# Sigmoid attention and a gated feed-forward on one core: the last gate on VectorE, sums issued earlier, the last copy in two halves

## The chip, the cores and the metric

The kernel runs on one core of one Trainium2 chip. The metric is the device time of one execution in microseconds (us). The core has five engines, each with an instruction queue of its own that is worked off in order: PE (TensorE, matmuls; its weight loads are the row PEld), DVE (VectorE), ACT (ScalarE), POOL (GpSimd) and SP (SyncE, which here only issues DMAs). An engine waits for another by semaphores. PSUM, which matmuls write, has 8 banks of 512 fp32 columns; SBUF holds everything else.

## The reference

With 8 batches, 12 heads, 448 tokens and a head size of 64, and then 3584 tokens of 768 features and 2048 hidden units:

```python
scores = scale * np.matmul(q, k.transpose(0, 1, 3, 2)) - np.log(S)
attn = 1.0 / (1.0 + np.exp(-scores))
x = np.matmul(attn, v)            # (8, 12, 448, 64), to (3584, 768) by token
h = x @ w_in                      # 768 -> 2048
g = h * (1.0 / (1.0 + np.exp(-beta * h)))
out = g @ w_out                   # 2048 -> 768
```

All inputs and the output are float32.

## The kernel before

Matmuls take fp16 operands. The attention is worked off by groups of four heads (24 groups of two score slots each, three groups to a batch). A **visit** (`visit`, L255) computes one key block's scores of a group: 8 or 16 short matmuls (L217) into four PSUM banks, and one sigmoid over all four (L245, on ACT, 1792 columns) that writes the attention weights to `attns`. The next visit's scores go to the same four banks, so they can start only when that sigmoid has read them. `attend` (L293) multiplies a group's weights with v (L304) and DVE copies the result to `xT` (L313). DVE also transposes q and k of the coming groups (L192, L200, L204), and doubles v's short last block (`double_v_last`, L157).

The two dense layers are the other half of PE's work. The first batches run plainly (`dense1`, `dense2`). From batch 2 on, two batches go together: `blocks(b, ...)` (L495), called for b = 2, 4 and 6 and called a **run** here, computes the first layer of batches b and b+1 by a seven-product Strassen scheme with 8 blocks i = 0..7 (`NB1` is 8). Each block leaves four results of 128 hidden units by 448 tokens. They are named A and B (the first batch, lower and upper half of the hidden units), D and E (the same of the second batch). A, B and D stand in PSUM; E is written by DVE to a scratch place in SBUF, inside `attns` (L553). `whole(key, i)` and `gate` (L486) finish a result: ACT computes the sigmoid into `sg` (L488), and one engine multiplies it with the result into the fp16 hidden tensor `gt` (L491). The multiplication of E is on POOL, that of A, B and D on DVE.

The second layer reads `gt` by tiles of 128 tokens. A run gives 7 tiles (`NTILE`), called a window: three pairs of tiles by seven products each (`strassen`, L584) and one tile alone (`single`, L375). Product i of a pair is 8 matmuls (dc = 0..7, `ND` is 8) of 384 columns, L593. Products 0 and 1 read `gt` itself; products 2 to 6 read a sum of two parts of `gt`, which `hidden_sum` makes on DVE (L582, fp16, 128x1024). The sum for product i+2 is issued within product i, at the matmul that the line L587 names. After products 1 to 6 ACT (L614) or DVE (L611, L616) takes the PSUM result into the output tile `osb`, and `store` (L633) issues its DMAs on SP.

The order of all work is written by hand (`tc.manual_schedule()`); each engine's queue holds its instructions in the order in which the Python code emits them. Matmuls of the dense layers lie in a list, `fill`, of which the main loop spends so many after each visit as a planned pace says. At a run, the main loop puts the new window at the end of `fill` but keeps the 8 last matmuls of the window before for use within the run. At its end, `blocks` emits, in this order:

```python
            if i:                                     # i == NB1 here
                whole("D", i - 1)()
            if i == NB1:
                share_psum(scores)
                other(2)                              # new window: product 0, dc 0 and 1
            if i:
                product1(b, i - 1, 4, kept[i - 1, "B"], False)
            if i:
                whole("B", i - 1)()
        other(ND - 2)                                 # product 0, dc 2 to 7; the sum at dc 4
        whole("E", NB1 - 1)()
```

After that come the visits of the main loop and, with them, products 1, 2 and so on. After the third run there are no visits left, and the second layer of the last window runs through to the end. The tile that comes last is tile 27 (`NT - 1`), which is computed alone: its right half is copied and stored first, its left half (`half == 0`) last, by `leave` (L363).

Of the kernel before, what the change touches and what calls it, by code (L numbers as in the profile page):

```python
# [13 lines left out]
def kernel(  # L14
# [10 lines left out]
    nc = tc.nc  # L25
# [17 lines left out]
    NB1 = DFF // P // 2  # L43
    NDC = DFF // P
    HALF = DM // 2
    WIN = 2 * S
    NTILE = WIN // P
# [25 lines left out]
    def share_psum(sc: int):  # L73

        scored[:] = [(2 * i, 2 * i + 1) for i in range(sc)]
        last = max(used.values())
        for i in range(2 * sc):
            used.pop(i, None)
        for i in range(2 * sc, 8):
            used.setdefault(i, last)  # L80

    def touch(i: int):
        used[i] = max(used.values(), default=0) + 1

    def bank(cols: int = S, hold=None, at=None):
        if at is None:
            at = min((i for i in used if i not in held.values()), key=used.get)
        assert at not in held.values()
        touch(at)
        if hold is not None:  # L90
            held[hold] = at
        width[at] = cols
        return ps[:, at, 0:cols]
# [222 lines left out]
    osbs = {}  # L316
# [27 lines left out]
    def release(key):  # L344
        touch(held.pop(key))
        m2s.pop(key)
# [16 lines left out]
    def leave(t: int, half: int, m2):  # L363
        lo, hi = half * HALF, (half + 1) * HALF
        release((t, half))
        if t not in osbs:
            osbs[t] = outp.tile([P, DM], FP32, tag="osb", name="osb")
        nc.vector.tensor_copy(out=osbs[t][:, lo:hi], in_=m2)
        left[t] = left.get(t, 0) + 1
        if t == NT - 1:  # L370
            store(t, lo, hi)
        elif left[t] == 2:
            store(t, 0, DM)
# [21 lines left out]
    NT = NTOK // P  # L395
# [5 lines left out]
    ND = NDC // 2  # L401
# [37 lines left out]
    def scratch(i: int, n: int):  # L439

        return attns[:, i : i + n].rearrange("p n h s -> p (n h s)")
# [21 lines left out]
    def product1(b: int, i: int, n: int, out, start: bool):  # L463

        x, y = xTs[b], xTs[b + 1]
        t1, t2, t3, t4 = xs[b]
        w, m = (
            (A11, x[:, 0:KH]),
            (A12, x[:, KH:]),
            (us["S4"], y[:, KH:]),  # L470
            (A22, t4),
            (us["S1"], t1),
            (us["S2"], t2),
            (us["S3"], t3),
        )[n - 1]
        for c in range(KH):
            nc.tensor.matmul(  # L477
                out,
                w[:, c, i * P : (i + 1) * P],
                m[:, c],  # L480
                start=(start and c == 0),
                stop=(c == KH - 1),
                skip_group_check=not start,
            )

    def gate(h, dc: int, b: int, engine):  # L486
        sg = sigp.tile([P, S], FP32, tag="sg", name="sg")
        nc.scalar.activation(  # L488
            out=sg, in_=h, func=AF.Sigmoid, bias=0.0, scale=beta_sb[:, dc : dc + 1]
        )  # L490
        return lambda: engine.tensor_tensor(  # L491
            out=gt[:, dc, b % 2 * S : b % 2 * S + S], in0=h, in1=sg, op=ALU.mult
        )

    def blocks(b: int, other, scores: int):  # L495

        kept = {}
        rest = sorted(used, key=used.get)
        firsts = [i for i in rest if width[i] == S and i not in held.values()][:2]
        others = sorted((i for i in rest if i not in firsts), key=lambda i: i in held.values())  # L500
        (b0, d0), (b2, d2) = scored
        share_psum(0)

        def take(key, i):
            at = firsts[i % 2] if key == "A" else ((b0, d0), others, (b2, d2))[i % 3][key == "D"]
            assert key != "A" or width[at] == S
            kept[i, key] = bank(S, (i, key), at)
            return kept[i, key]

        def whole(key, i):  # L510
            h = kept.pop((i, key))
            if (i, key) in held:
                touch(held.pop((i, key)))
            half, second = {"A": (0, 0), "D": (0, 1), "B": (1, 0), "E": (1, 1)}[key]
            return gate(h, i + half * NB1, b + second, nc.gpsimd if key == "E" else nc.vector)

        for i in range(NB1 + 1):
            p5 = scratch(6 + i % 2, 1).bitcast(FP32)
            if i < NB1:
                B = take("B", i)  # L520
                product1(b, i, 1, B, True)
                A = take("A", i)
                nc.scalar.copy(out=A, in_=B)
                D = take("D", i)
                product1(b, i, 5, D, True)
                nc.scalar.copy(out=p5, in_=D)
            if i:
                product1(b, i - 1, 3, kept[i - 1, "D"], False)
            if 0 < i < NB1:
                late = whole("E", i - 1)  # L530
            if i == 0:
                other(ND // 2)
            if i < NB1:
                product1(b, i, 6, B, False)
                nc.vector.tensor_tensor(out=D, in0=B, in1=p5, op=ALU.add)  # L535
            if 0 < i < NB1:
                late()
            if i:
                whole("D", i - 1)()
            if i < NB1:  # L540
                product1(b, i, 2, A, False)
                whole("A", i)()
            if i == 0:
                other(ND // 2)
            if i == NB1:
                share_psum(scores)
                other(2)
            if i:
                product1(b, i - 1, 4, kept[i - 1, "B"], False)
            if i < NB1:  # L550
                product1(b, i, 7, B, False)
                E = kept[i, "E"] = scratch(8 + i % 2, 1).bitcast(FP32)
                nc.vector.tensor_tensor(out=E, in0=B, in1=p5, op=ALU.add)  # L553
            if i:
                whole("B", i - 1)()
        other(ND - 2)
        whole("E", NB1 - 1)()
# [17 lines left out]
    NPROD = 7  # L575
# [8 lines left out]
    def strassen(t: int, i: int, dc: int):  # L584

        name, x, _, op, w = product(t, i)
        if dc == (0 if i else ND // 2) and i + 2 < NPROD:  # L587
            hidden_sum(t, i + 2)
        first = (t, name) not in m2s
        if first:  # L590
            m2s[t, name] = bank(HALF, (t, name))
        m2 = m2s[t, name]
        nc.tensor.matmul(  # L593
            m2,
            (x if op is None else sums[t, i])[:, dc],
            w[:, dc],
            start=first,
            stop=(dc == ND - 1),
            skip_group_check=i >= 4,
        )  # L600
        if dc < ND - 1:
            return
        if i == 0:
            for u in (t, t + 1):
                osbs[u] = outp.tile([P, DM], FP32, tag="osb", name="osb")
        L, R = slice(0, HALF), slice(HALF, DM)
        o1, o2 = osbs[t], osbs[t + 1]
        r, a = m2s.get((t, "r")), m2s.get((t, "a"))

        def add(out, in0, in1, op=ALU.add):  # L610
            nc.vector.tensor_tensor(out=out, in0=in0, in1=in1, op=op)  # L611

        if i == 1:
            nc.scalar.copy(out=o2[:, L], in_=a)  # L614
        elif i == 2:
            nc.vector.tensor_copy(out=o1[:, L], in_=m2)  # L616
            add(o1[:, R], r, o1[:, L])
            release((t, "s"))
        elif i == 3:
            add(o2[:, L], m2, o2[:, L])  # L620
            release((t, "b"))
        elif i == 4:
            add(o2[:, R], a, o2[:, L], ALU.subtract)
        elif i == 5:
            add(o2[:, R], r, o2[:, R])
            release((t, "r"))
            store(t + 1, 0, DM)
        elif i == 6:
            add(o1[:, L], a, o1[:, L], ALU.subtract)
            release((t, "a"))  # L630
            store(t, 0, DM)

    def store(t: int, lo: int, hi: int):  # L633
        osb = osbs[t]
        c, end = t * P, (t + 1) * P
        while c < end:
            b, i = divmod(c, S)
            rows = out[b * S : (b + 1) * S, lo:hi]
            if b == B - 1:
                n = min(end - c, S - i)  # L640
                to = rows[i : i + n]
            else:
                n = BLK
                to = rows.rearrange("(p c) m -> c p m", c=NB)[i // BLK]
            nc.sync.dma_start(out=to, in_=osb[c - t * P : c - t * P + n, lo:hi])
            c += n
# [269 lines left out]
```

## Time and profile before

| | |
|---|---|
| median of 3 runs | 381.13 us (381.05 to 381.13) |
| profiled execution, its own time | 381.19 us |
| its span, from the first to the last instruction | 379.4 us |
| granted TensorE clock | 1.000 |
| PE busy | 370.7 us (98% of the span) |
| DVE busy | 256.8 us (68%) |
| ACT busy | 258.4 us (68%) |
| POOL busy | 94.7 us (25%) |
| runs (first layer of two batches) | 133 to 168, 222 to 257, 309 to 345 us from the span's start |
| last window | 345 to 376 us |

The profile is one execution, taken by the hardware profiler. In its views a row of the timeline has a start and a duration in us, the engine, the line, the operation, what it writes and reads, and how many instructions are merged; in brackets stands how long the engine sat idle before and for whom. Matmuls are pipelined: the record of one ends later than the next begins, so what counts is the distance from start to start. In the view of waits a row reads: who waited, for whom, us in total, times, the longest.

### The profile page before, as it was taken

The page shows a single profiled execution, that of the slowest core. Times are in us where ns is not written, and L with a number is a line of the kernel's source. Part 1 is how long each engine was busy: PE and PEld are TensorE (multiplying, and loading weights), DVE is VectorE, ACT ScalarE, POOL GpSimd, SP SyncE. Part 2 cuts the span into 40 slices and gives each one's busy share as a digit, 9 for nine tenths or more (in the row PEclk, how much of TensorE's full clock was granted, in tenths as well). Part 3 has the DMA queues.
Part 4 walks back from the last instruction along what each step waited for, and adds up shares of the span by engine and source line. Part 5 has one row for each costly group of instructions (what it writes and reads, how often), then busy time and mean ns, then how long its engine had stood idle before and what let it go on. Part 6 is the DMA issues. An engine that isn't in the chain of part 4 may idle for free.

```text
span 379.4 us, 7379 instructions
## 1 busy us (share of the span) xinstructions
PE 370.7 (98%) x2927; PEld 186.2 (49%) x2927; DVE 256.8 (68%) x483; ACT 258.4 (68%) x303; POOL 94.7 (25%) x141
## 2 busy tenths in 40 slices
PE   8999999999999999999999999999999999999996
PEld 3467664444444455544444445554444445555663
DVE  3256686776687786787576666778667567678662
ACT  3987776688977758887767658887677737882000
POOL 7833353141141012335114003227100002231000
PEclk9999999999999999999999999999999999999999
DMA  7999999993339030009739311007903031000333
GB/s 113 177 187 203 197 205 198 214 126 56 50 54 185 18 83 1 2 2 167 152 65 198 76 44 30 2 0 112 194 0 85 7 78 42 2 0 3 83 83 126
DMA packets 42403, 34.31 MB, mean 90 GB/s; under 512 B 21873, under 2 KB 38913, under 8 KB 42369
## 3 DMA queue, kind: packets, MB, share of 16 engines
q0 software_dynamic: 36976, 22.81, 44.2%
q1 hardware_dynamic: 5392, 11.02, 10.3%
q8 instruction: 23, 0.38, 0.4%
q14 instruction: 12, 0.09, 0.1%
HBM read 45.62 MB, written 11.01 MB: 149 GB/s over the span
## 4 chain that ended last, share of the span: by engine, by line
PE 91%; DVE 5%; ACT 3%; issue 1%; ACTq 0%
PE ps L477 25%; PE ps L593 25%; PE ps L217 12%; PE ps L304 10%; PE ps L324 9%; PE ps L353 4%; PE ps L391 4%; PE ps L712 3%; DVE sum L582 1%; ACT attns L230 1%; DVE xT L313 1%; ACT sg L488 1%; DVE ps L535 1%; DVE w_S L437 1%; DVE gt L491 1%
## 5 line engine op out<-in xcount | busy, mean ns | idle before, releaser
L245 ACT ACTIVATE attns<-ps,nlogs 128x1792 f16<-128x1792 f32 x73 | 128.0, 1753 | 49.3 <-PE ps L217 49.1
L491 POOL TENSOR_TENSOR gt<-attns,sg 128x448 f16<-128x448 f32 x24 | 27.3, 1137 | 151.3 <-ACT sg L488 151.3
L593 PEld LDWEIGHTS <-sum 128*128 128x128 f16 x440 | 39.9, 98 | 38.0 <-issue 11.6
L217 PE MATMUL ps<-qT,kT 32*128 32x448 f16 (+3 forms) x864 | 51.8, 340 | 1.3 <-ACT attns L230 0.6
L488 ACT ACTIVATE sg<-ps,beta_sb 128x448 f32<-128x448 f32 x72 | 45.4, 631 | 8.0 <-PE ps L477 5.8
L593 PE MATMUL ps<-w_T,sum 128*128 128x384 f16 x264 | 49.1, 327 | 0.0
L477 PE MATMUL ps<-xT,w_S 128*128 128x448 f16 x216 | 48.7, 352 | 0.2
L477 PE MATMUL ps<-xT,w_in 128*128 128x448 f16 x216 | 48.7, 353 | 0.0
L313 DVE CAST xT<-ps 128x448 f16<-128x448 f32 (+1 forms) x54 | 28.7, 567 | 27.3 <-PE ps L304 27.2
L491 DVE TENSOR_TENSOR gt<-ps,sg 128x448 f16<-128x448 f32 x72 | 44.6, 619 | 1.4 <-ACT sg L488 1.0
L324 PE MATMUL ps<-xT,w_in 128*128 128x224 f16 (+1 forms) x288 | 40.5, 291 | 1.2 <-ACT attns L230 0.8
L304 PE MATMUL ps<-attns,v 128*64 128x448 f16 (+3 forms) x432 | 41.3, 340 | 0.0
L477 PEld LDWEIGHTS <-w_in 128*128 128x128 f16 x288 | 28.0, 98 | 26.3 <-issue 0.4
L611 DVE TENSOR_TENSOR osb<-ps,osb 128x384 f32<-128x384 f32 x55 | 30.5, 555 | 13.2 <-PE ps L593 11.2
L582 DVE TENSOR_TENSOR sum<-gt 128x1024 f16<-128x1024 f16 x55 | 38.9, 729 | 0.2
L126 POOL DMA_DIRECT2D raw<-in_q_dram x27 | 15.0, 557 | 76.5 <-DVE kT L204 66.7
L593 PE MATMUL ps<-w_out,sum 128*128 128x384 f16 x176 | 32.4, 327 | 1.5 <-DVE sum L582 1.1
L338 DVE TENSOR_TENSOR gt<-ps,sg 128x224 f16<-128x224 f32 (+1 forms) x48 | 21.1, 465 | 18.2 <-ACT sg L335 18.2
L593 PE MATMUL ps<-w_out,gt 128*128 128x384 f16 x176 | 33.3, 327 | 0.0
L324 PEld LDWEIGHTS <-w_in 128*128 128x128 f16 x288 | 26.4, 98 | 14.0 <-issue 6.6
L535 DVE TENSOR_TENSOR ps<-ps,attns 128x448 f32<-128x448 f32 x24 | 15.2, 632 | 24.4 <-PE ps L477 24.4
L477 PEld LDWEIGHTS <-w_S 128*128 128x128 f16 x216 | 21.1, 98 | 20.1 <-issue 0.9
(49 smaller groups left out, 376.0 us busy)
## 6 DMA issues: line engine op xcount, KB each, us to landing
out_dram<-osb SPq DMA_DIRECT2D x98, 96.0 KB, 1.9
raw<-in_k_dram POOLq DMA_DIRECT2D x24, 224.0 KB, 5.4
raw<-in_q_dram POOLq DMA_DIRECT2D x21, 224.0 KB, 4.3
v<-in_v_dram POOLq DMA_DIRECT2D x32, 144.0 KB, 6.9
w_in<-in_moe_w_in_dram POOLq DMA_DIRECT2D x8, 384.0 KB, 10.8
w_out<-in_moe_w_out_dram POOLq DMA_DIRECT2D x4, 768.0 KB, 13.6
v<-in_v_dram POOLq DMA_DIRECT2D x16, 48.0 KB, 6.5
out_dram<-osb SPq DMA_DIRECT2D x2, 384.0 KB, 2.6
```

Of the source, the lines that this page charges most:

```text
L217: nc.tensor.matmul(sco[base : base + nk, hh, u0 : u0 + n], kT[g][lo : lo + BLK, jt * P : jt * P + nk, e], qT[g][lo : lo + BLK, c0 : c0 + n ...
L245: nc.scalar.activation(out=attns[:, slot : slot + 2].rearrange("p n h s -> p (n h) s"), in_=sco, func=AF.Sigmoid, bias=nlogs[:, 0:1], scal ...
L304: nc.tensor.matmul(av[hh * D : (hh + 1) * D, 0:n], vs[b][base : base + nk, 2 * (s % NPAIR) + hh, jt], at[base : base + nk, hh, 0:n], start ...
L313: nc.vector.tensor_copy(out=xTs[b][:, s % NPAIR, c0 : c0 + n], in_=av[:, 0:n])
L324: nc.tensor.matmul(m1, w_in16[:, hc, dc * P : (dc + 1) * P], xTs[b][:, hc, c0 : c0 + n], start=(hc == 0), stop=(hc == NHC - 1),)
L338: nc.vector.tensor_tensor(out=gt[:, dc, off : off + n], in0=m1, in1=sg[:, 0:n], op=ALU.mult)
L477: nc.tensor.matmul(out, w[:, c, i * P : (i + 1) * P], m[:, c], start=(start and c == 0), stop=(c == KH - 1), skip_group_check=not start,)
L488: nc.scalar.activation(out=sg, in_=h, func=AF.Sigmoid, bias=0.0, scale=beta_sb[:, dc : dc + 1])
L491: return lambda: engine.tensor_tensor(out=gt[:, dc, b % 2 * S : b % 2 * S + S], in0=h, in1=sg, op=ALU.mult)
L582: nc.vector.tensor_tensor(out=sums[t, i], in0=x, in1=y, op=op)
L593: nc.tensor.matmul(m2, (x if op is None else sums[t, i])[:, dc], w[:, dc], start=first, stop=(dc == ND - 1), skip_group_check=i >= 4,)
L611: nc.vector.tensor_tensor(out=out, in0=in0, in1=in1, op=op)
```

## The change

There are three edits. First, in each run, E of the last block (i = 7) is multiplied on DVE; E of blocks 0 to 6 stays on POOL. It is still emitted at the same place, after the six matmuls and the sum among them. Second, in the pairs that do not open a window, the sum for product 2 is issued at the first matmul of product 0 and no more at its fifth, four matmuls earlier; these are eight pairs (tiles 3, 5, 9, 11, 16, 18, 23 and 25). The pairs that open a window (tiles 7, 14 and 21) keep the fifth. Third, the last PSUM copy of the kernel, 384 columns on DVE, becomes one of 192 columns on DVE and one of 192 columns on ACT; both read the same PSUM bank.

```diff
@@ leave
-        nc.vector.tensor_copy(out=osbs[t][:, lo:hi], in_=m2)
+        if t == NT - 1 and half == 0:
+            mid = HALF // 2
+            nc.vector.tensor_copy(out=osbs[t][:, lo : lo + mid], in_=m2[:, 0:mid])
+            nc.scalar.copy(out=osbs[t][:, lo + mid : hi], in_=m2[:, mid:])
+        else:
+            nc.vector.tensor_copy(out=osbs[t][:, lo:hi], in_=m2)
@@ blocks, whole
-            return gate(h, i + half * NB1, b + second, nc.gpsimd if key == "E" else nc.vector)
+            return gate(h, i + half * NB1, b + second, nc.gpsimd if key == "E" and i < NB1 - 1 else nc.vector)
@@ strassen
-        if dc == (0 if i else ND // 2) and i + 2 < NPROD:
+        if dc == (ND // 2 if i == 0 and t % NTILE == 0 else 0) and i + 2 < NPROD:
             hidden_sum(t, i + 2)
```

## The prediction

> **What bounds the kernel now.** I read the page's chain first: it is PE's, with a small share of DVE in a line of sums.
>
> ```profile
> PE 91%; DVE 5%; ACT 3%; issue 1%; ACTq 0%
> ```
>
> So an edit counts only where it makes PE go on earlier, or shortens what follows PE's last matmul. The waits say where PE waits for sums:
>
> ```profile
> PEld L593 <- DVE sum L582: 2.2, 3, 1.1
> ...
> PE ps L593 <- DVE sum L582: 1.1, 3, 0.8
> ```
>
> Three times in all, of 55 sums. The sums' own line gives the shortest, median and longest duration in ns:
>
> ```profile
> L582 DVE TENSOR_TENSOR sum<-gt x55: 641/683/1620, 103.8 to 367.8; 128x1024 f16<-128x1024 f16 x55
> ```
>
> A few sums take 1.62 us for 0.68. The timeline around the end of the third run shows what lies beside one:
>
> ```profile
> 342.76 2.44 PE L593 MATMUL ps<-w_out,gt 128*128 128x384 f16 x14
> ...
> 343.49 0.66 ACT L488 ACTIVATE sg<-attns,beta_sb 128x448 f32<-128x448 f32 x1
> 343.62 0.62 DVE L491 TENSOR_TENSOR gt<-ps,sg 128x448 f16<-128x448 f32 x1 [0.32 <-ACT sg L488]
> 344.23 1.13 POOL L491 TENSOR_TENSOR gt<-attns,sg 128x448 f16<-128x448 f32 x1 [3.30 <-ACT sg L488]
> 344.28 2.82 DVE L582 TENSOR_TENSOR sum<-gt 128x1024 f16<-128x1024 f16 x3
> ...
> 345.95 6.13 PEld L593 LDWEIGHTS <-sum 128*128 128x128 f16 x39 [1.15 <-DVE sum L582]
> 345.96 2.77 PE L593 MATMUL ps<-w_out,sum 128*128 128x384 f16 x16 [0.76 <-DVE sum L582]
> ```
>
> POOL's multiplication of E starts at 344.23, the sum for product 2 at 344.28. The chain in order of time gives this sum 1.63 us, to 345.91: it ends 0.55 after POOL (345.36), about what a sum takes alone. It looks as if DVE stood still until POOL was done. At the end of the first run the same pair lies among visits (the second run, at 256.56, repeats it to 0.01 us):
>
> ```profile
> 168.11 1.13 POOL L491 TENSOR_TENSOR gt<-attns,sg 128x448 f16<-128x448 f32 x1 [3.31 <-ACT sg L488]
> 168.17 1.62 DVE L582 TENSOR_TENSOR sum<-gt 128x1024 f16<-128x1024 f16 x1
> ...
> 168.22 1.47 PE L593 MATMUL ps<-w_out,gt 128*128 128x384 f16 x8
> 168.34 1.75 ACT L245 ACTIVATE attns<-ps,nlogs 128x1792 f16<-128x1792 f32 x1 [0.31 <-PE ps L217]
> ...
> 169.85 0.66 PE L593 MATMUL ps<-w_out,sum 128*128 128x384 f16 x3 [0.15 <-DVE sum L582]
> ...
> 170.44 0.57 PE L217 MATMUL ps<-qT,kT 32*128 32x448 f16 x8
> ```
>
> Last, prices, by shape:
>
> ```profile
> L491 DVE TENSOR_TENSOR gt<-ps,sg 128x448 f16<-128x448 f32 x72 | 44.6, 619 | 1.4 <-ACT sg L488 1.0
> ...
> L368 DVE COPY osb<-ps 128x384 f32<-128x384 f32 x12 | 6.7, 555 | 13.3 <-PE ps L391 7.7 <-PE ps L353 5.5
> ...
> L313 DVE CAST xT<-ps 128x224 f16<-128x224 f32 x12 | 4.4, 387 | 4.5 <-PE ps L304 4.5
> ```
>
> **E of the last block on DVE: third run.** Matmuls of L593 follow each other every 0.164 us (16 from 345.96 to the next product's start at 348.57). The 14 before the stall therefore fill PE from 342.76 to 345.06, and product 2 starts at 345.96: 0.90 lost. With POOL idle the sum runs 344.28 to 344.96; PE took up its work 0.05 after the sum's end (345.91 to 345.96), so it may start at 345.01 and PE's own 345.06 decides. In the unstalled stream weight loads lead their matmul by some 0.19 (342.57 against 342.76), and this one leads by 0.05 only, so I take 0.02 off: gain **0.88**.
>
> What is late next? The multiplication now follows that sum on DVE, ahead of the sum for product 3. The trace has none on DVE from SBUF; the nearest row is the same instruction with one operand in PSUM, 0.62; POOL's own 1.13 is the far end. Its sigmoid ended at 344.15, so it does not wait. At 0.62: multiplication 344.9 to 345.5, next sum to 346.2, wanted by PE at 345.06 + 8 x 0.164 = 346.37. It fits by 0.1 or so. At 1.13 it would be 0.4 late and the gain 0.5. I take 0.62. Below 0.62 nothing more is gained. No reader is near: E belongs to the second batch, which the window's second pair opens, 56 matmuls later.
>
> **First and second run.** The 8 matmuls from 168.22 end their turn at 169.53, the sum would be there at 168.85, PE went on at 169.85: 0.32, and 0.31 in the second run (257.98 against 258.29). Behind it waits the next visit, whose scores need the banks that ACT's sigmoid reads until 168.34 + 1.75 = 170.09. PE would get there at 170.44 - 0.32 = 170.12, just after. From then on ACT and PE turn in step: the second sigmoid, at 171.07, waited for those scores, moves with them, and frees the third visit, so I count the gain as carried on: **0.31 twice**. On DVE the k transposes and the sum for product 3 stand behind the multiplication. Before, they stood behind 1.62 us; now behind 0.68 + 0.62 = 1.30, so they are 0.3 early, as PE is. On POOL the next q and k loads stood behind the multiplication (one begins at 169.19, without a wait) and can go after block 6's E (ends 164.81), some 4 us earlier. The DVE work there multiplies fp32 from PSUM and ran beside POOL's earlier E gates at its usual 0.62, so I price this at nothing; if a DVE row were held for one 0.55 us issue per run, PE still would not wait for it.
>
> **Sums four matmuls earlier.** Outside the three places PE never waits for a sum, so there is nothing to gain. In the trace's order only matmuls lie between the first and fifth matmul in five of the eight pairs, and in tile 3's pair a visit without DVE work: the DVE queue stays as it is. In two (visits at 197.94 and 286.25) the doubling of v's last block (0.35) stands there and now comes one sum, 0.68, later; the products with that v come at 211.66 and 299.22, over 12 us on. Without that cover it would cost up to 2 x 0.68; I take **0**. No DMA moves with it.
>
> **The last copy.** A DVE copy is 0.555 for 384 columns; the casts' 0.619 for 448 and 0.387 for 224 give 1.04 ns a column, so 192 take 0.36. ACT's copies are 0.517 for 448 (L523) and 0.474 for 384 (L614): 0.67 ns a column, 0.35 for 192. Side by side the stage shrinks from 0.56 to 0.36: gain 0.20. One after the other, with 0.03 between as from ACT's sigmoid to DVE's multiplication, it is 0.74: loss 0.18. Nowhere in this trace do both engines read one bank at once: ACT's sigmoid and DVE's multiplication of a block follow each other (342.96 + 0.63, then 343.62). That is by their data, but it is the nearest row, and I take the loss, **-0.18**, with both ends kept. The two DMAs now wait for ACT too; the wait is in the 0.18.
>
> The Trainium skill's page "PSUM — Partial Sum Buffer", section "PSUM bank collisions raise a hardware error", speaks against this edit: two engines on one bank and the same partitions at once, two reads included, collide, the hardware doesn't arbitrate, so they have to be kept apart by semaphores. By that rule the sum would hold -0.18, without it +0.20; no row here shows such an overlap.
>
> **Sum.** 0.88 + 0.62 + 0 - 0.18 = 1.32 us. The profiled execution took 381.19 (379.4 of span and 1.8 around it), 0.06 above the median of the runs: 379.87 for it, **379.8** against the median of 381.13.
>
> **Rivals.**
>
> *The halves run side by side* (0.30): 381.13 - 1.70 = 379.4. For it: they write different columns and neither needs the other. Against: the missing overlap.
>
> *The first two gains are not carried on* (0.08). Visits are close to ACT's limit: scores at 172.87 start 0.05 after the sigmoid's end (171.07 + 1.75). If the turn between them doesn't shift, 0.62 is lost: 380.4 (380.05 with parallel halves). Against it: just there ACT waited for PE.
>
> *The sum stays long* (0.07), because something other than POOL holds it. Then the multiplication only lengthens DVE's queue, the sum for product 3 ends at about 347.2, before PE wants it (347.27): 381.1 to 381.3. Against: the three long sums are the three with POOL beside them, to the same 0.06 us.
>
> *DVE blocked behind ACT: slower* (0.05). A gate on DVE blocks everything behind it if its sigmoid is late. Were that sigmoid queued behind the visit's 1.75 us one, it would end at 170.09 + 0.67 = 170.76; multiplication 0.62, k transposes 0.57 and 0.20, sum 0.68: 172.83, while PE wants that sum at 171.46 (5 matmuls after the visit, which ends at 170.64). PE stalls 1.4 and nets 1.1 lost in each of two runs: 381.13 + 2.2 - 0.88 + 0.18 = 382.6. It decides once the sigmoid ends after about 169.4. Against: it is issued before the visit and starts at 167.38.
>
> **How the numbers follow.** The forecast has 0.50. A measurement of this kernel can tell about 0.2%, 0.76 us. The forecast, the parallel halves and a third of the lost carry are beyond it: 0.83 faster. The rest of the lost carry and the long sum make 0.12 for the same; the blocked DVE 0.05 slower. The range takes in the forecast, the parallel halves (379.4, less some hundredths for the weight load), the lost carry and a slow multiplication in the third run (1.13: 380.2 to 380.3): 379.3 to 380.5, with 0.12 left out.
>
> **What would show it.** Right: no sum over 0.75 us; no wait of L593 for L582; in the third run product 2 starts 2.30 after its 14 matmuls; 72 + 3 multiplications on DVE and 21 on POOL, those three at 0.6; two rows of 192 columns at the end, ACT's starting when DVE's ends. Wrong: a sum still at 1.6; a new wait of L593 for the sum of product 3; visits in the first two windows not 0.3 earlier; k transposes that make L217 wait.

## The result and the profile after

The changed kernel takes 379.67 us in the median of 7 runs (379.4 to 379.9), the kernel before 381.05 in the median of 7. The ratio is 0.9968, with a 95% interval of 0.9958 to 0.9977: faster by 0.3%, 1.4 us by the medians. The profiled execution took 379.55 us; its span is 377.6. The ratios of the later experiments leave out one execution of the kernel before, of 726.5 us, which was in a slow state.

The chain of waits of the changed kernel has lost the sums, and PE's share has gone from 91 to 93%:

```profile
PE 93%; DVE 3%; ACT 2%; issue 1%; ACTq 0%
PE ps L598 27%; PE ps L482 25%; PE ps L217 12%; PE ps L304 10%; PE ps L324 9%; PE ps L353 4%; PE ps L396 4%; PE ps L717 2%; ACT attns L230 1%; DVE xT L313 1%; DVE ps L540 1%; DVE w_S L442 1%; ACT sg L335 0%; ACT attns L245 0%; DVE qT L192 0%
```

(Lines have moved by five: the sums are now L587, the second layer L598, the gate's multiplication L496. In the kernels of the experiments they move by other amounts.) The line of the sums and the multiplications by shape:

```profile
L587 DVE TENSOR_TENSOR sum<-gt x55: 647/681/693, 103.5 to 365.9; 128x1024 f16<-128x1024 f16 x55
```

```profile
L496 DVE TENSOR_TENSOR gt<-attns,sg 128x448 f16<-128x448 f32 x3 | 1.8, 616 | 0.0
```

The longest of 55 sums is 0.69 us, where it was 1.62, and the three new multiplications on DVE are 0.62 each. The timeline of the third run's end, in the same order as before:

```profile
341.76 2.44 PE L598 MATMUL ps<-w_out,gt 128*128 128x384 f16 x14
...
343.29 0.69 DVE L587 TENSOR_TENSOR sum<-gt 128x1024 f16<-128x1024 f16 x1
343.90 0.62 DVE L496 TENSOR_TENSOR gt<-attns,sg 128x448 f16<-128x448 f32 x1
344.03 5.96 PEld L598 LDWEIGHTS <-sum 128*128 128x128 f16 x38 [0.22 <-DVE sum L587]
344.04 2.77 PE L598 MATMUL ps<-w_out,sum 128*128 128x384 f16 x16
...
344.43 1.28 DVE L587 TENSOR_TENSOR sum<-gt 128x1024 f16<-128x1024 f16 x2
```

Product 2 starts 2.28 us after the first of the 14 matmuls ahead of it (341.76 to 344.04), where it was 3.20. A weight load still waits 0.22 for the sum, PE itself no more. The sum for product 3 follows the multiplication and is done about 345.1, 0.2 before PE takes it up at 344.04 + 1.31 = 345.35.

The end of the kernel:

```profile
373.78 0.33 PE L396 MATMUL ps<-w_out,sum 128*128 128x384 f16 x1
374.15 0.36 DVE L370 COPY osb<-ps 128x192 f32<-128x192 f32 x1 [0.74 <-PE ps L396]
374.54 0.32 ACT L371 COPY osb<-ps 128x192 f32<-128x192 f32 x1 [11.61 <-DVE osb L370]
```

The halves do not run side by side: ACT's starts 0.03 us after DVE's has ended, and the profile names DVE's copy as what ACT waited for. The stage is 0.71 us long, where one copy took 0.56.

**Where the time went, stage by stage.** Each run contains one unbroken stretch of 153 first-layer matmuls, 29.10 us in every trace, and the chain lists its start; it also lists the start of the last tile's 32 matmuls. These marks cut all traces of this study alike: from the first stretch to the second, from the second to the third, from the third to the last tile, and from there to the end of the last copy. For the kernel before, the marks and the last copy are:

```profile
136.76 29.10 PE ps L477 x153
...
225.21 29.10 PE ps L477 x153
...
312.88 29.10 PE ps L477 x153
...
370.83 5.21 PE ps L391 x32
```

```profile
376.07 0.56 DVE L368 COPY osb<-ps 128x384 f32<-128x384 f32 x1 [0.74 <-PE ps L391]
```

For the changed kernel the marks are:

```profile
136.44 29.10 PE ps L482 x153
...
224.59 29.10 PE ps L482 x153
...
311.88 29.10 PE ps L482 x153
...
368.91 5.21 PE ps L396 x32
```

The differences, in us (the experiments of the lower rows follow below):

| kernel | first to second run | second to third | third to last tile | last tile to last copy's end | sum, against before |
|---|---|---|---|---|---|
| before | 88.45 | 87.67 | 57.95 | 5.80 | |
| changed | 88.15 | 87.29 | 57.03 | 5.95 | -1.45 |
| first edit alone | 88.15 | 87.30 | 57.04 | 5.80 | -1.58 |
| second edit alone | 88.46 | 87.65 | 57.96 | 5.80 | 0.00 |
| third edit alone | 88.45 | 87.66 | 57.96 | 5.95 | +0.15 |
| first edit, last copy on ACT | 88.15 | 87.31 | 57.04 | 5.72 | -1.65 |
| E on POOL in two halves | 88.16 | 87.38 | 57.50 | 5.79 | -1.04 |
| third run's E on POOL, later | 88.15 | 87.30 | 57.04 | 5.71 | -1.67 |
| first edit, two banks | 88.15 | 87.30 | 57.04 | 5.59 | -1.79 |
| first edit, last copy on ACT, POOL kept busy | 88.15 | 87.30 | 62.10 | 5.72 | +3.40 |

A stage repeats to 0.02 us between traces that share its code. What lies ahead of the first mark does not: it was reached at 136.76 before and 136.44 after, and between 135.94 and 136.90 in the ten traces. Only the second edit reaches into that part (tiles 3 and 5), and it changes the order of no instruction there. So 0.32 us of the difference between the two traces lie ahead of the first mark and owe nothing to the change; with the 1.45 of the stages they make 1.77, about the difference of the spans (379.4 and 377.6). The profiled executions' own times differ by 1.64, since a little more time lay around the span in the second.

### The profile page after: what moved, and what is told of

It reads as the page before. It is cut to its first block, busy times and chain, and to the rows that moved or that the text cites. A ratio compares the mean times of both kernels' runs of the same rounds, so it can differ in the third digit from the quotient of the medians.

```text
span 377.6 us, 7384 instructions
## 1 busy us (share of the span) xinstructions
PE 369.9 (98%) x2927; PEld 186.3 (49%) x2927; DVE 255.2 (68%) x486; ACT 258.9 (69%) x304; POOL 91.5 (24%) x138
## 4 chain that ended last, share of the span: by engine, by line
PE 93%; DVE 3%; ACT 2%; issue 1%; ACTq 0%
PE ps L598 27%; PE ps L482 25%; PE ps L217 12%; PE ps L304 10%; PE ps L324 9%; PE ps L353 4%; PE ps L396 4%; PE ps L717 2%; ACT attns L230 1%; DVE xT L313 1%; DVE ps L540 1%; DVE w_S L442 1%; ACT sg L335 0%; ACT attns L245 0%; DVE qT L192 0%
## 5 line engine op out<-in xcount | busy, mean ns | idle before, releaser
L496 POOL TENSOR_TENSOR gt<-attns,sg 128x448 f16<-128x448 f32 x21 | 23.9, 1140 | 141.2 <-ACT sg L493 141.2
L598 PEld LDWEIGHTS <-sum 128*128 128x128 f16 x440 | 40.0, 98 | 36.3 <-issue 11.6
L598 PE MATMUL ps<-w_T,sum 128*128 128x384 f16 x264 | 49.0, 327 | 0.0
L496 DVE TENSOR_TENSOR gt<-ps,sg 128x448 f16<-128x448 f32 x72 | 44.5, 618 | 1.5 <-ACT sg L493 1.0
L587 DVE TENSOR_TENSOR sum<-gt 128x1024 f16<-128x1024 f16 x55 | 36.3, 678 | 0.2
L598 PE MATMUL ps<-w_out,gt 128*128 128x384 f16 x176 | 33.3, 327 | 0.0
L598 PE MATMUL ps<-w_out,sum 128*128 128x384 f16 x176 | 32.3, 327 | 0.4 <-DVE xT L313 0.4
```

The lines of the kernel that those rows point to most:

```text
L496: return lambda: engine.tensor_tensor(out=gt[:, dc, b % 2 * S : b % 2 * S + S], in0=h, in1=sg, op=ALU.mult)
L587: nc.vector.tensor_tensor(out=sums[t, i], in0=x, in1=y, op=op)
L598: nc.tensor.matmul(m2, (x if op is None else sums[t, i])[:, dc], w[:, dc], start=first, stop=(dc == ND - 1), skip_group_check=i >= 4,)
```

## The experiments

Theory: POOL's multiplication holds up the fp16 sum that DVE starts beside it; moving it to DVE removes the three long sums; the second edit is worth nothing; the two halves of the last copy go one after the other, because they lie in one PSUM bank. Rivals: the gain comes from the earlier sums; the long sums had another cause; the halves are apart for another reason. The kernel before was run again beside each of the two sets of experiments; its medians there are 380.85 us (up to `act_copy`) and 381.22 us (from `pool_halves` on).

**Each edit alone.** First the gate (`only_gate`):

```diff
-            return gate(..., nc.gpsimd if key == "E" else nc.vector)
+            return gate(..., nc.gpsimd if key == "E" and i < NB1 - 1 else nc.vector)
```

> The kernel before with the first edit alone: E of each run's last block multiplied on VectorE. Theory (POOL's multiplication holds the fp16 sum beside it): the whole gain and a little more than the full change, 0.9 in the third run and 0.3 in each of the others, about -1.5 us against before; no sum over 0.75 us, no wait of product 2 for its sum. Rival (the gain comes from the earlier sums, or the runs among visits give theirs back): -0.9 or less.

Measured: 379.22 us against 380.85, ratio 0.9957 (0.9944 to 0.9969). The stages give -1.58, of which 0.30, 0.37 and 0.91 in the three windows: the whole gain of the change, and 0.13 more. As the theory expected; the rival is out.

Then the sums alone (`only_sums`):

```diff
-        if dc == (0 if i else ND // 2) and i + 2 < NPROD:
+        if dc == (ND // 2 if i == 0 and t % NTILE == 0 else 0) and i + 2 < NPROD:
```

> The kernel before with the second edit alone: in eight pairs the sum for product 2 is issued four matmuls earlier. Theory: only two neighbours on VectorE's queue change places (a sum and the doubling of v's last block), for whose end nobody waits: 0.0 us against before, within 0.1 in the trace; the three sums of 1.62 us are still there. Rival (earlier sums hide some of the waits): -0.3 us or more.

Measured: 380.89 against 380.85, ratio 0.9998 (0.9988 to 1.0007); all four stages as before to 0.02 us. The instruction order of the two kernels differs on DVE's queue alone, in just two places, where a sum and L157 change places. The sums' line keeps its long ones:

```profile
L582 DVE TENSOR_TENSOR sum<-gt x55: 640/681/1621, 103.5 to 367.5; 128x1024 f16<-128x1024 f16 x55
```

The last copy alone (`only_copy`):

```diff
+        if t == NT - 1 and half == 0:
...
+            nc.vector.tensor_copy(out=osbs[t][:, lo : lo + mid], in_=m2[:, 0:mid])
+            nc.scalar.copy(out=osbs[t][:, lo + mid : hi], in_=m2[:, mid:])
...
```

> The kernel before with the third edit alone: the last PSUM copy in two halves on VectorE and ScalarE. Theory (the halves of one bank are kept apart): ScalarE's half starts 0.03 us after VectorE's ends, the stage from PE's last matmul to the last store's issue grows from 0.59 to about 0.74 us, the time by +0.15 us against before. Rival (the halves overlap when the rest of the kernel is as before): the stage is 0.39 us and the time -0.2 us.

Measured: 381.21 against 380.85, ratio 1.0008 (0.9999 to 1.0016): the times alone leave it open. The stage does not: 5.95 for 5.80, with nothing else changed.

```profile
376.02 0.36 DVE L370 COPY osb<-ps 128x192 f32<-128x192 f32 x1 [0.74 <-PE ps L396]
376.41 0.32 ACT L371 COPY osb<-ps 128x192 f32<-128x192 f32 x1 [11.61 <-DVE osb L370]
```

One after the other again. The third edit costs 0.15 us.

**The copy undivided on ACT** (`act_copy`), with the first edit:

```diff
+        if t == NT - 1 and half == 0:
+            nc.scalar.copy(out=osbs[t][:, lo:hi], in_=m2)
...
```

> The first edit, and the last copy undivided on ScalarE in place of the two halves; the second edit left out. Theory (a copy of 384 columns is 0.47 us on ScalarE, 0.56 on VectorE and 0.71 in two halves one after the other): -0.24 us against the changed kernel, -0.08 against the first edit alone, so about -1.6 us against before, below both. Rival (ScalarE, idle for over 10 us, starts late or slowly): no better than the first edit alone.

Measured: 379.24, ratio 0.9956 (0.9943 to 0.9968), level with the first edit alone (379.22). In the trace the copy is 0.48 us on ACT and the stage 5.72 for 5.80: the 0.08 are there, but lie below what the times can tell.

**Is it POOL that holds the sum?** E stays on POOL, cut in two (`pool_halves`):

```diff
...
+        if engine is nc.gpsimd and dc == NDC - 1:
+            return lambda: (times(0, QH), times(QH, QH))
...
```

(`times` multiplies a stretch of columns, here 224 each.)

> The kernel before, with E of each run's last block still on POOL but as two instructions of 224 columns. Theory (VectorE's fp16 sum stands still for the one POOL instruction beside which it starts, and no longer): the sum for product 2 takes about 0.6 + 0.5 = 1.1 us for 1.62, product 2 of the third run starts 0.5 us earlier than before, those of the first two runs without a stall (0.3 each): about -1.1 us against before. Rival (the two engines share the memory in some proportion, or POOL's second half goes first): the sum still takes about 1.6 us and the time is that of before.

Measured: 380.22 against 381.22, ratio 0.9977 (0.9967 to 0.9986). The first run's end:

```profile
168.25 1.73 POOL L492 TENSOR_TENSOR gt<-attns,sg 128x224 f16<-128x224 f32 x2 [3.30 <-ACT sg L488]
168.31 1.15 DVE L587 TENSOR_TENSOR sum<-gt 128x1024 f16<-128x1024 f16 x1
```

The sum takes 1.15 for 1.62, and so follows the length of the one POOL instruction beside which it starts: the first half alone takes 0.66 us, 0.47 less than the whole 1.13, and the sum is shorter by the same 0.47. POOL pays too: the two halves take 1.73 us, where a whole multiplication takes 1.14, and the second half, which finds the sum running, is the longer one (1.11). The stages give -1.04 of the 1.1 expected. The rival is out.

**POOL beside work from PSUM** (`pool_late`). With the first edit and the last copy on ACT, E of the third run goes back to POOL, eight matmuls later (`blocks` returns the step of E instead of taking it):

```diff
...
-        first_layer(B - 2)
+        last = first_layer(B - 2)
+        fill_units(ND)
+        last()
```

> The first edit in the first two runs only; in the third, E of the last block is multiplied on POOL after all, but issued eight matmuls later, so that POOL's 1.1 us lie beside VectorE's copy and addition out of PSUM and beside no sum. The last copy is undivided on ScalarE. Theory (only VectorE's fp16 work from SBUF is held): copy and addition keep their 0.56 us, no sum is over 0.75 us, PE waits for none, and the time is that of the kernel with all three E on VectorE and the copy on ScalarE, about -1.6 us against before. Rival (any VectorE instruction beside POOL's multiplication is held): a copy or addition of 1.1 us or more.

Measured: 379.53, ratio 0.9956 (0.9944 to 0.9968), and the stages of `act_copy` to 0.01 us:

```profile
344.88 1.13 POOL L494 TENSOR_TENSOR gt<-attns,sg 128x448 f16<-128x448 f32 x1 [5.44 <-ACT sg L491]
345.06 0.56 DVE L621 COPY osb<-ps 128x384 f32<-128x384 f32 x1 [0.36 <-PE ps L598]
345.66 0.56 DVE L616 TENSOR_TENSOR osb<-ps,osb 128x384 f32<-128x384 f32 x1
```

Both of DVE's instructions out of PSUM keep their 0.56 us beside POOL's 1.13. So the multiplication need not leave POOL; in the third run, where this was tried, it is enough that it doesn't lie beside the sum.

**POOL kept busy** (`pool_busy`): sixteen multiplications of scratch data, which nothing reads, beside the last window (with the first edit and the last copy on ACT):

```diff
...
+        for _ in range(16):
+            nc.gpsimd.tensor_tensor(out=busy[2], in0=busy[0], in1=busy[1], op=ALU.mult)
```

> The first edit and the last copy on ScalarE, and POOL kept busy in the third run's end and the last window by 16 extra fp32 multiplications of scratch data (448 columns, some 1.14 us each, 18 us in all), which nothing waits for. Theory: sums that start beside one take up to 1.7 us and PE waits for several of them, so some 2 to 8 us more than without; VectorE's work that reads PSUM keeps its 0.56 to 0.62 us. Open: whether the fp32 multiplication of E on VectorE, both operands in SBUF, is held as well (0.62 or over 1 us). Rival (the three long sums had another cause): sums of 0.68 us throughout and the time unchanged.

Measured: one run, of 384.72 us. By the stages it is 5.05 longer than `act_copy`, all of it in the stretch with the extra work (62.10 for 57.04), and inside the 2 to 8 us expected. The same place in the third run, a later sum, and POOL's multiplications one by one (shortest, median and longest in ns):

```profile
340.72 21.52 POOL L892 TENSOR_TENSOR attns<-attns 128x448 f32<-128x448 f32 x15
...
342.52 0.62 DVE L494 TENSOR_TENSOR gt<-ps,sg 128x448 f16<-128x448 f32 x1 [0.32 <-ACT sg L491]
343.18 1.64 DVE L585 TENSOR_TENSOR sum<-gt 128x1024 f16<-128x1024 f16 x1
...
344.75 1.54 DVE L494 TENSOR_TENSOR gt<-attns,sg 128x448 f16<-128x448 f32 x1
344.88 1.47 PE L596 MATMUL ps<-w_out,sum 128*128 128x384 f16 x8 [0.79 <-DVE sum L585]
346.22 3.15 DVE L585 TENSOR_TENSOR sum<-gt 128x1024 f16<-128x1024 f16 x2
...
350.34 0.68 DVE L585 TENSOR_TENSOR sum<-gt 128x1024 f16<-128x1024 f16 x1
```

```profile
L892 POOL TENSOR_TENSOR attns<-attns x16: 1129/1458/1578, 340.7 to 362.3; 128x448 f32<-128x448 f32 x16
```

The multiplication with an operand in PSUM keeps 0.62 us (342.52). The sum takes 1.64, and the same multiplication with both operands in SBUF 1.54 (344.75): it is held as well, in fp32. POOL's own multiplications go from 1.13 to 1.58, with a median of 1.46, where one alone takes 1.14: each side waits for the other. Who started first keeps its time: the sum at 350.34 takes its 0.68, and it is the multiplication that POOL starts at 350.43 that takes 1.58. This is what the Trainium skill's page "SBUF — State Buffer", section "SBUF: two separate sides", states: VectorE and GpSimd share a pair of SBUF ports, held for a whole instruction by whichever starts first, and a VectorE instruction with two SBUF inputs needs it against a GpSimd instruction that reads SBUF. The rows agree with it: VectorE's instructions with two SBUF inputs are held (1.64 and 1.54 us), those with one are not (0.62), and the wait falls on the later of the two.

**Why the halves were apart** (`two_banks`): with the first edit, the last half tile is computed as 2 x 192 columns in two banks, with twice as many matmuls.

```diff
+            for to, lo in ((m2, 0), (m2s[t, "x"], mid)):
+                nc.tensor.matmul(to[:, 0:mid], x[:, dc], w[:, dc, lo : lo + mid], ...)
...
+                nc.vector.tensor_copy(out=osbs[t][:, 0:mid], in_=m2[:, 0:mid])
+                nc.scalar.copy(out=osbs[t][:, mid:HALF], in_=second[:, 0:mid])
...
```

> The first edit, and the last half tile computed as two times 192 columns in two PSUM banks, by 32 matmuls for 16; VectorE copies the one, ScalarE the other. Theory (the halves of the change were kept apart because they lie in one bank): both copies start within 0.05 us of PE's end, the stage is 0.36 us for 0.71 in two halves of one bank; the 32 matmuls of 192 columns cost 0 to 0.6 us more (the 224-column ones of the first layer came every 0.10 us), so -0.2 to +0.4 us against the first edit alone. Rival (ScalarE waits for VectorE for another reason): ScalarE's copy again starts only when VectorE's ends.

Measured: 379.07 us, ratio 0.9949 (0.9937 to 0.9962), the lowest ratio of the study, below that of the changed kernel (0.9968) too, though the two intervals overlap a little.

```profile
372.42 1.48 PE L396 MATMUL ps<-w_out,sum 128*128 128x192 f16 x16
...
373.86 0.36 DVE L401 COPY osb<-ps 128x192 f32<-128x192 f32 x1 [0.68 <-PE ps L396]
373.94 0.32 ACT L402 COPY osb<-ps 128x192 f32<-128x192 f32 x1 [11.26 <-PE ps L396]
```

ACT is now released by PE and starts 0.08 us after DVE, about the distance of one matmul (0.082), as its bank is written last. The 16 matmuls of 192 columns take 1.48 us, 8 of 384 took 1.46 to 1.47: doubling them costs nothing to speak of. The two copies together last 0.40 us (373.86 to 374.26). The stage is 5.59 for 5.80 with one copy on DVE and 5.95 with two halves of one bank; 0.05 of the gain is that DVE's copy can start earlier, as its bank is done before the last matmul. Same halves, same engines, other bank: the bank made them wait. It was not the data, for the halves of one bank share no column, and not the tile, for all eight banks are one tile of the program (`ps`). The Trainium skill's page "PSUM — Partial Sum Buffer" ("PSUM bank collisions raise a hardware error") asks for two engines to be kept apart on one bank. The program does so, by a wait; no run here shows what an overlap would do.

## Why the prediction was right

**The third run.** Forecast 0.88; the stage shrank by 0.92. The working held step by step: sum 0.69 (0.68), multiplication 0.62 (taken from the row with one operand in PSUM), product 2 after 2.28 (2.30 was PE's own pace), the next sum done 0.2 ahead of its use (0.1). The 0.02 set aside for the late weight load was not needed: the load waited 0.22, though no wait of this line for a sum was expected, and PE lost nothing.

**The first two runs.** Forecast 0.31 each and carried to the end; measured 0.30 and 0.38. They were carried: visits and ACT's sigmoids moved with PE, and the rival of a lost carry falls. In the second window 0.07 more was gained than the stall is long, and the traces place 0.06 of it at one visit. Before, ACT's sigmoid there starts 0.69 after its scores (266.30 to 266.99); in the changed kernel it starts 0.63 after them (265.38 to 266.01), and in both the next visit follows that sigmoid's end by 0.05 (268.79 and 267.81). The forecast had no such term. Why ACT was later there before stays open. The first run's end, with the visit that was feared to wait for ACT:

```profile
168.02 1.75 ACT L245 ACTIVATE attns<-ps,nlogs 128x1792 f16<-128x1792 f32 x1 [0.31 <-PE ps L217]
168.46 0.62 DVE L496 TENSOR_TENSOR gt<-attns,sg 128x448 f16<-128x448 f32 x1
...
169.21 0.65 PE L598 MATMUL ps<-w_out,sum 128*128 128x384 f16 x3
...
169.82 0.57 PE L217 MATMUL ps<-qT,kT 32*128 32x448 f16 x8
```

Product 2 starts 1.31 after its 8 matmuls (167.90), the visit's scores at 169.82, 0.05 after the sigmoid that frees their banks (169.77). The multiplication's sigmoid ended at 167.71, 0.75 before the multiplication started, so the rival of a blocked DVE queue falls as well.

**POOL's loads.** The next q load moved from 169.19 to 164.43, as worked out, and the DVE instructions beside it, which read PSUM, kept 0.62 to 0.63. Nothing lost.

**The sums.** Forecast 0, with two swaps on DVE's queue; measured 0.00, with those two swaps.

**The last copy.** The forecast took a loss of 0.18 from the nearest row and kept a gain of 0.20 as the other end. The loss is 0.15: ACT's 192 columns took 0.32 and not 0.35. The row that the loss was taken from was a weak ground, since its order comes from the data; that the halves wait for each other because of their bank was shown only by `two_banks`. The gain of 0.20 was found only with another bank (`two_banks`, 0.21).

**The sum.** 1.32 was forecast, 379.8 us; the median is 379.67, with the kernel before at 381.05 in these runs and not 381.13, so by the medians the gain is 1.38. By the stages it is 1.45, so the terms together were 0.13 too small: 0.07 in the second window, 0.04 in the third run and 0.03 in the copy, less 0.01 in the first window.

## What to carry to other kernels

When a few instances of an instruction take more than twice their median, look at what every other engine does in just those moments: here three of 55 gave stalls worth 1.6 us, and the culprit was off the critical path. The remedy is to change neighbours, not necessarily engines: VectorE's work with an operand in PSUM lay beside GpSimd unharmed (0.56 and 0.62 us). And here splitting a copy between two engines paid only with the halves in different PSUM banks; in one bank it cost 0.15 us.

## What the runs showed beyond what was expected

A 192-column matmul with its own weight load came every 0.082 us, half of the 384-column one, where the nearest row of before (224 columns every 0.10 us) had left up to 0.6 us of cost open for 32 of them. When they meet, POOL loses time as well as DVE: POOL's multiplication took up to 1.58 us for 1.14, a sum up to 1.64 for 0.68. And the start of this kernel, up to the first run's mark, varies by almost 1 us between the traces, more than the smaller edits are worth: differences of some tenths were told apart by stages between fixed marks, not by whole times.
